# Global queries' scores between a head's two local score visits, with 128 weight columns and one key layout for both products

## The chip, the cores and the metric

The kernel runs on one core of a Trainium2 chip. The metric is the device time of one launch in microseconds. The core has TensorE (matrix products, written to PSUM), VectorE and ScalarE (both read PSUM and SBUF), GpSimd (SBUF only here) and SyncE, which issues the DMAs. In the profile they are PE (with PEld for its weight loads), DVE, ACT, POOL and SP. Each engine takes its instructions in the order of its own queue; semaphores hold an instruction back until what it needs has happened on another engine.

## The reference

Sparse attention followed by a gated feed-forward net. There are 8 batches of 8 heads, 512 local tokens, 32 global tokens and head width 64. Global queries see all 544 keys; a local query sees the 32 global keys and the local keys at most 32 positions away.

```python
k_all = np.concatenate([k_g, k_l], axis=2)
s_g = scale * np.matmul(q_g, k_all.transpose(0, 1, 3, 2))
out_g = np.matmul(sm(s_g), v_all)
...
s_ll = np.where(np.abs(pos[:, None] - pos[None, :]) <= 32, s_ll, -1000000000.0)
s_l = np.concatenate([s_lg, s_ll], axis=-1)
out_l = np.matmul(sm(s_l), np.concatenate([v_g, v_l], axis=2))
...
gate = 1.0 / (1.0 + np.exp(-(x @ w_gate)))
return (gate * (x @ w_val) @ w_out).astype(np.float32)
```

`sm` is softmax over the last axis. The 4352 tokens x of width 512 (eight heads of 64) run through a net with 1536 hidden columns.

## The kernel before

**Two streams are woven into one program.** The feed-forward net is a stream of items, one for each 128 hidden columns of a chunk of 512 tokens: 12 long products into a `bank_g`, 12 into a `bank_v` (L400), then 12 for the output of the item before (L437). After every four products the stream yields; that is one unit of time, nine units an item. The attention of the chunk that the net will need next is a list of events with due times in these units (`att_events`, L449); after each yield the events that are due are written into the program. The framework then orders the instructions for each engine by its own estimates and gives out the buffers, so an engine's queue need not follow the written order exactly.

**A head.** In the steady part a head takes 12 units (PER = 4 for each of two local units and for the global part). Local unit 0 handles query blocks 0 and 1, unit 1 blocks 2 and 3. A unit has four stages at 0, 3, 6 and 9 units after its start (`STAGES`), and unit 1 starts 4 units after unit 0:

- the scores (L239), four products into one bank, then mask and minimum on VectorE (L253) and the exponential on ScalarE (L256);
- sum and reciprocal (L259, L260) and four normalisations into `p_buf` on VectorE (L223);
- four transposes into a `bank_y` (L271), which ScalarE rounds (L282, high part) and VectorE subtracts (L283, low part) into `pt`;
- four output products (L301, L302), read by L304 and L305.

**The global part.** `global_scores` (L308) is due 8 units after the head's start. Its weights are the 32 global queries; two pairs of products run over the local keys (L318) and one pair over the 32 global keys (L320), into two banks. ScalarE copies both into the head's 32 rows of `pg` (L322, L323). After every fourth head `global_group` takes the softmax of the 128 rows (L330 to L335), transposes them (L340, 6 units later) and multiplies by the values (L361, 9 units later).

**Precision.** All products of the steady part are float32r, with an operand split in a rounded high and a low part. `split_qk` (L196) does this for queries and keys: a cast on ScalarE (L202), a subtraction for the keys (L203) and two for the queries (L205) on GpSimd. There are two `qk_hi` buffers and one `qk_raw`: a head's cast can start when the head two before has made its last product from its `qk_hi`. The first chunks, while the weights are still being converted, use plain float32 (heads called native; 12 of those with a global part). The other 52 heads are split heads.

**Buffers.** The banks `bank_x`, `bank_y`, `bank_g` and `bank_v` share four PSUM banks. A new one gets a bank that an older one has given up, and TensorE waits until the last reader of that older one is through.

**Layout.** The host lays the keys out in four groups of 160: 64 local keys, the 32 global keys, 64 local keys, with 32 keys of margin ahead (`host_layout`, L562; KEXT = 704 columns); queries 0 to 255 stand before, the others and then the global queries behind.

Heads are numbered 0 to 7 within a batch below. The period of 12 units against the item's nine gives three phases; heads 1, 4, 7 have one, 2 and 5 another, 3 and 6 the third. Groups end at heads 3 and 7.

Of the kernel before, what the change touches and what calls it, by code (L numbers as in the profile page):

```python
# [8 lines left out]
F32 = mybir.dt.float32  # L9
# [8 lines left out]
P = 128  # L18
D = 64
SL = 512  # L20
SG = 32
NH = 8
BLK = 160
KEXT = 4 * BLK + 64
K0 = 256
Q1 = K0 + KEXT
QK = Q1 + 256 + SG
# [3 lines left out]
KALL = SL + SG  # L31
# [5 lines left out]

BASE, PER = 3, 4
STAGES = (0, 3, 6, 9)
GSTAGES = (0, 6, 9)  # L40
LOAD_QK, LOAD_V, SPLIT_QK, SPLIT_V = 16, 9, 10, 4
LOAD_V_NATIVE = 4

# [16 lines left out]
def kernel(ctx, tc, qk, v, w_gate, w_val, w_out, out_l, out_g):  # L60
    nc = tc.nc
# [7 lines left out]
    att = ctx.enter_context(tc.tile_pool(name="att", bufs=2))  # L69
# [4 lines left out]
    ps = ctx.enter_context(tc.tile_pool(name="ps", bufs=1, space=PSUM))  # L74
# [18 lines left out]
    pg = const.tile([P, 5 * P], F32, name="pg_buf")  # L93
# [214 lines left out]
    def global_scores(T, row):  # L308
        ks, k0s, q0 = T["qk"], T["k0"], T["q0"]
        last = len(ks) - 1  # L310
        qg = ks[0][:, QK - SG - q0:QK - q0]
        sa = ps.tile([SG, 4, P], F32, name="bank_x", tag="att", bufs=4)
        sb = ps.tile([SG, SG], F32, name="bank_y", tag="att", bufs=4)
        for half in range(2):
            o0 = 96 * half
            for t, (src, k0) in enumerate(zip(ks, k0s)):
                view = src[:, k0 + 32:k0 + 32 + 4 * BLK].rearrange("p (j c) -> p j c", c=BLK)[:, :, o0:o0 + 64]
                nc.tensor.matmul(sa[:, :, 64 * half:64 * half + 64], qg, view, start=t == 0, stop=t == last)  # L318
        for t, (src, k0) in enumerate(zip(ks, k0s)):
            nc.tensor.matmul(sb, qg, src[:, k0 + 96:k0 + 128], start=t == 0, stop=t == last)  # L320
        rows = slice(SG * row, SG * (row + 1))
        nc.scalar.copy(pg[rows, 0:SL], sa.rearrange("p a c -> p (a c)"))  # L322
        nc.scalar.copy(pg[rows, SL:KALL], sb)  # L323

    def global_group(Ts, b, g):

# [122 lines left out]
    def att_events(ci, start, per, tail=0):  # L449
# [4 lines left out]
        nu = len(blocks) // 2  # L454
# [5 lines left out]
        for h in range(NH):  # L460
            native = ci + 1 if ci < 2 or (ci == 2 and h < START["native_heads"]) else 0
            place = (spl, "qk_hi", QK)
            if ci == 0 and h >= 4:
                place = (spl, "kl", KEXT)
            if ci == 1 and h // 2 == 2:
# [11 lines left out]
        for h in range(NH):  # L477
            T = heads[h]
            base = start + per * npu * h
            sc = per / 4  # L480
            ev.append((base - sc * LOAD_QK, 0, lambda T=T: load_qk(T)))
            ev.append((base - sc * (LOAD_V_NATIVE if T["native"] else LOAD_V), 0, lambda T=T: load_v(T)))
            ev.append((base - sc * SPLIT_QK, 1, lambda T=T: split_qk(T)))
            ev.append((base - sc * SPLIT_V, 1, lambda T=T: split_v(T)))
            for i in range(npu):
                t0 = base + per * i
                if i == nu:
                    ev.append((t0, 2, lambda T=T, h=h: global_scores(T, h % GH)))
                    if h % GH < GH - 1:
                        continue  # L490
                for o in STAGES if i < nu else GSTAGES:
                    ev.append((t0 + sc * o, 2, lambda h=h, i=i: adv(h, i)))
            if h % 2 == 1:
                ev.append((base + (nu - 1) * per + sc * STAGES[-1] + 0.5, 3,
                           lambda kt=h // 2: x_split(xts[ci], x32s[kt], kt, x0, ntok)))
# [27 lines left out]
    for ci in range(3, G):  # L523
        at, width = HOLE
        t0 = 9 * NF * (ci - 2)
# [36 lines left out]
def host_layout(inputs):  # L562
# [6 lines left out]
    kg = k_g.reshape(N, SG, D)  # L569
    ke = np.zeros((N, KEXT, D), np.float32)  # L570
    vl = v_l.reshape(N, SL, D)
    vg = v_g.reshape(N, SG, D)
    ve = np.zeros((N, 8, P, D), np.float32)
    for j in range(4):
        o = 32 + j * BLK
# [13 lines left out]
    c = np.ascontiguousarray  # L589
# [27 lines left out]
```

## Time and profile before

| | us |
|---|---|
| three timed runs | 1200.74, 1204.21, 1206.13 |
| the profiled execution | 1199.83 |
| its span, first to last instruction | 1197.8 |
| idle time of TensorE in the span | 37.1 |
| L400 into `bank_g` and `bank_v`, busy | 332.9 and 329.3 |
| L437, busy | 329.0 |
| L318 and L320 together, busy in split heads | 26.9 + 26.8 + 9.5 + 9.4 |
| L202 on ScalarE, one cast of 128x1248 | 1.24 |
| L203 on GpSimd, one subtraction of 128x704 | 1.70 |

The idle time is the span less TensorE's busy 1160.7. Products are pipelined, so the time from one start to the next is what counts for TensorE, not the length of one row. A row of the timeline gives start, length, engine, line, operation, output and inputs, shapes and the number of merged instructions; in brackets stands how long the engine was idle before it and what ended the wait. The DMA queue that carries all data was busy 41.6% of its 16 engines' time.

### The profile page before, as it was taken

To read this page: it belongs to the slowest core of one execution; us is meant where nothing else is said; L and a number is where in the kernel's file an instruction comes from. 1 tells how busy PE (TensorE), PEld (TensorE's weight loads), DVE (VectorE), ACT (ScalarE), POOL (GpSimd) and SP (SyncE) were. 2 spreads that over 40 slices of the span, in tenths; PEclk is the share of its full clock that TensorE was granted. 3 is DMA by queue.
4 is the path that set the end of the run, shared out by engine and by line. 5 is a ranking of instruction groups with operands and counts; after the bars stand their busy time and mean duration, and the time that the engine had idled before them with its cause. 6 is when DMAs were issued, how large, how long until landed. Compare 5 with 4: busy or idle time off the path is not lost.

```text
span 1197.8 us, 19349 instructions
## 1 busy us (share of the span) xinstructions
PE 1160.7 (97%) x6652; PEld 973.6 (81%) x6652; DVE 807.5 (67%) x2186; ACT 753.0 (63%) x1719; POOL 417.3 (35%) x408
## 2 busy tenths in 40 slices
PE   8889999999999999999999999999999999999998
PEld 6667778888888888888888888888888888888897
DVE  6889966766776776766776776667776677633343
ACT  5777777756765676766676666666666666532333
POOL 1335344524442444424442444424443444100000
PEclk9889999999999999999999999999999999999999
DMA  8787854333433432433343433443433332131143
GB/s 288 243 261 225 262 169 139 109 102 97 119 97 116 127 113 85 126 118 114 100 110 115 121 98 108 114 127 96 114 113 102 114 114 66 53 106 64 60 143 121
DMA packets 59489, 151.81 MB, mean 127 GB/s; under 512 B 6144, under 2 KB 19456, under 8 KB 59392
## 3 DMA queue, kind: packets, MB, share of 16 engines
q1 hardware_dynamic: 59392, 150.59, 41.6%
q8 instruction: 52, 0.85, 0.3%
q14 instruction: 45, 0.37, 0.1%
HBM read 135.36 MB, written 15.20 MB: 126 GB/s over the span
## 4 chain that ended last, share of the span: by engine, by line
PE 72%; DVE 10%; ACT 5%; issue 2%; POOL 1%; DMA 0%; DVEq 0%; ACTq 0%; POOLq 0%
PE bank_v L400 19%; PE bank_g L400 19%; PE bank_o L437 19%; PE bank_y L271 3%; DVE p_buf L223 3%; PE bank_x L239 3%; ACT s_sb L256 2%; PE bank_x L301 2%; PE bank_x L302 2%; PE bank_x L318 2%; PE bank_x L361 1%; DVE bank_v L420 1%; DVE pt L283 1%; DVE bank_v L421 1%; DVE mn L413 1%
## 5 line engine op out<-in xcount | busy, mean ns | idle before, releaser
L400 PE MATMUL bank_v<-xt,wv 128*128 128x512 f32 (+1 forms) x1440 | 329.3, 365 | 11.8 <-DVE pt L283 11.8
L400 PE MATMUL bank_g<-xt,wg 128*128 128x512 f32 (+1 forms) x1440 | 332.9, 366 | 0.2 <-ACT pg_buf L322 0.2
L437 PE MATMUL bank_o<-wo,hh 128*128 128x512 f32 x1224 | 329.0, 400 | 0.9 <-ACT hh L423 0.4
L400 PEld LDWEIGHTS bank_v<-xt,wv 128*128 128x128 f32 x1440 | 238.2, 190 | 49.3 <-PE bank_y L320 12.6
L400 PEld LDWEIGHTS bank_g<-xt,wg 128*128 128x128 f32 x1440 | 238.8, 191 | 37.6 <-issue 3.2
L437 PEld LDWEIGHTS bank_o<-wo,hh 128*128 128x128 f32 x1224 | 217.2, 189 | 40.8 <-ACT hh L423 1.4
L256 ACT ACTIVATE s_sb<-s_sb,nm 128x192 f32<-128x192 f32 (+1 forms) x240 | 110.7, 462 | 102.6 <-DVE nm L253 102.2
L223 DVE TENSOR_SCALAR p_buf<-s_sb,r 128x128 f32<-128x128 f32 (+2 forms) x443 | 145.8, 370 | 7.6 <-PE bank_y L271 1.9
L216 POOL TENSOR_TENSOR vhl<-v_raw,vhl 128x512 fp32r<-128x512 f32 x52 | 67.8, 1304 | 193.4 <-ACT vhl L215 108.1
L306 POOL TENSOR_TENSOR x<-t 64x256 f32<-64x256 f32 x104 | 76.2, 733 | 165.5 <-DVE t L305 125.2
L203 POOL TENSOR_TENSOR kl<-qk_raw,qk_hi 128x704 fp32r<-128x704 f32 x52 | 88.6, 1704 | 112.0 <-ACT qk_hi L202 111.5
L423 ACT CAST hh<-bank_v 128x512 fp32r<-128x512 f32 (+1 forms) x120 | 62.7, 522 | 95.9 <-DVE bank_v L421 95.1
L408 ACT ACTIVATE th<-bank_g 128x512 f32<-128x512 f32 (+1 forms) x120 | 63.7, 531 | 89.5 <-PE bank_g L400 88.9
L413 DVE TENSOR_SCALAR mn<-bank_g 128x512 f32<-128x512 f32 (+1 forms) x108 | 67.5, 625 | 73.2 <-ACT th L408 73.2
L305 DVE TENSOR_TENSOR t<-bank_x,t 64x512 f32<-64x512 f32 x104 | 70.8, 681 | 62.1 <-ACT t L304 61.3
L420 DVE TENSOR_TENSOR bank_v<-bank_v,mn 128x512 f32<-128x512 f32 (+1 forms) x120 | 73.7, 614 | 52.7 <-PE bank_v L400 45.9
L253 DVE CUSTOM_DVE_ANT_0 s_sb<-bank_x,masks 128x192 f32<-128x192 f32 (+1 forms) x240 | 80.8, 370 | 38.7 <-PE bank_x L239 35.8
L424 DVE TENSOR_TENSOR hh<-bank_v,hh 128x512 fp32r<-128x512 f32 (+1 forms) x120 | 73.0, 608 | 39.8 <-ACT hh L423 39.2
L271 PE MATMUL bank_y<-ident,p_buf 128*128 128x128 f32 x496 | 76.7, 275 | 6.6 <-DVE p_buf L223 5.6
L205 POOL TENSOR_TENSOR qk_hi<-qk_raw,qk_hi 64x256 fp32r<-64x256 f32 x104 | 80.4, 794 | 4.1
L271 PEld LDWEIGHTS bank_y<-ident,p_buf 128*128 128x128 f32 x496 | 60.5, 141 | 22.8 <-DVE p_buf L223 5.7
L283 DVE TENSOR_TENSOR pt<-bank_y,pt 128x512 fp32r<-128x512 f32 x104 | 70.9, 682 | 7.3 <-ACT pt L282 7.1
(110 smaller groups left out, 1707.8 us busy)
## 6 DMA issues: line engine op xcount, KB each, us to landing
wo<-wo_dram SPq DMA_DIRECT2D x116, 512.0 KB, 3.5
qk_raw<-in_qk_dram SPq DMA_DIRECT2D x104, 312.0 KB, 4.4
v_raw<-in_v_dram SPq DMA_DIRECT2D x52, 256.0 KB, 2.6
out_dram<-ob SPq DMA_DIRECT2D x34, 256.0 KB, 3.1
xt<-in_w_gate_dram SPq DMA_DIRECT2D x12, 512.0 KB, 4.9
xt<-in_w_val_dram SPq DMA_DIRECT2D x12, 512.0 KB, 4.6
xt<-in_w_out_dram SPq DMA_DIRECT2D x12, 512.0 KB, 4.5
v_nat<-in_v_dram SPq DMA_DIRECT2D x8, 512.0 KB, 6.0
```

What stands on the lines that cost most here:

```text
L203: nc.gpsimd.tensor_tensor(kl, t[:, K0:Q1], hi[:, K0:Q1].bitcast(F32), op=ALU.subtract)
L205: nc.gpsimd.tensor_tensor(hi[64:128, r], t[64:128, r], hi[64:128, r].bitcast(F32), op=ALU.subtract)
L223: nc.vector.tensor_scalar(out, in_, by, None, op0=ALU.mult)
L253: anchor[0] = nc.vector.tensor_tensor_reduce(out=s_sb[:, i, w], in0=s_ps[:, i, w], in1=mid[:, w], scale=-0.125, scalar=3.0e38, op0=ALU.add ...
L256: exp_at[0] = nc.scalar.activation(s_sb[:, i, w], s_sb[:, i, w], AF.Exp, bias=nm[:, i:i + 1], scale=-1.0, accum_out=sm[:, i:i + 1])
L271: nc.tensor.transpose(pt_ps[:, 2 * i + t], pb[:, i, t * P:(t + 1) * P], ident)
L283: nc.vector.tensor_tensor(pt[:, 1], pt_ps, pt[:, 0].bitcast(F32), op=ALU.subtract)
L306: nc.gpsimd.tensor_tensor(dst, t0[:, :, 0], t0[:, :, 1], op=ALU.add)
L400: nc.tensor.matmul(acc, w[a][:, t, fs], xt[:, c, t, x0:x0 + ntok], start=n == 0, stop=n == 11)
L413: nc.vector.tensor_scalar(mn, acc, 0.0, None, op0=ALU.min)
L420: nc.vector.tensor_tensor(acc, acc, mn, op=ALU.mult)
L437: nc.tensor.matmul(o_ps[t], ph[:, a, t * P:(t + 1) * P], pwo[:, c], start=f2 == 0 and i == 0, stop=f2 == NF - 1 and i == 2)
```

## The change

The global scores of a head are due 3 units after its start (`GLOBAL_AT`), between the scores of unit 0 (at 0) and of unit 1 (at 4), where they were due after 8. The group's stages follow at 0, 5 and 8 units from there, before 0, 6 and 9.

The weights are now the last 128 query columns, 96 local queries and the 32 global ones, so the result has 128 rows, of which the last 32 are used. The keys get a fifth part at their end, the 32 global keys again and 32 zeros (KEXT = 736, so a `qk` tile has 1280 columns in place of 1248). The first product pair runs over the first 64 keys of all four groups and this fifth part, 320 columns; the second over the last 64 of each group, 256 columns. The pair of 32 columns is gone. Each pair has a bank of its own and a copy of its own into `pg`.

```diff
-KEXT = 4 * BLK + 64
+KEXT = 4 * BLK + 3 * 32
-GSTAGES = (0, 6, 9)
+GLOBAL_AT, GSTAGES = 3, (0, 5, 8)
...
-        qg = ks[0][:, QK - SG - q0:QK - q0]
-        sa = ps.tile([SG, 4, P], F32, name="bank_x", tag="att", bufs=4)
-        sb = ps.tile([SG, SG], F32, name="bank_y", tag="att", bufs=4)
-        for half in range(2):
-            o0 = 96 * half
+        qg = ks[0][:, QK - P - q0:QK - q0]
+        rows = slice(SG * row, SG * (row + 1))
+        for half, n in enumerate((5, 4)):
+            sg = ps.tile([P, n, 64], F32, name="bank_x", tag="att", bufs=4)
             for t, (src, k0) in enumerate(zip(ks, k0s)):
-                view = src[:, k0 + 32:k0 + 32 + 4 * BLK].rearrange("p (j c) -> p j c", c=BLK)[:, :, o0:o0 + 64]
-                nc.tensor.matmul(sa[:, :, 64 * half:64 * half + 64], qg, view, start=t == 0, stop=t == last)
-        for t, (src, k0) in enumerate(zip(ks, k0s)):
-            nc.tensor.matmul(sb, qg, src[:, k0 + 96:k0 + 128], start=t == 0, stop=t == last)
-        rows = slice(SG * row, SG * (row + 1))
-        nc.scalar.copy(pg[rows, 0:SL], sa.rearrange("p a c -> p (a c)"))
-        nc.scalar.copy(pg[rows, SL:KALL], sb)
+                k = src[:, k0 + 32 + 96 * half:k0 + 96 + 96 * half]
+                view = bass.AP(k.tensor, k.offset, [k.ap[0], (BLK, n), (1, 64)])
+                nc.tensor.matmul(sg, qg, view, start=t == 0, stop=t == last)
+            nc.scalar.copy(pg[rows].rearrange("p (j c) -> p j c", c=P)[:, 0:n, 64 * half:64 * half + 64], sg[P - SG:])
...
-                t0 = base + per * i
+                t0 = base + (per * i if i < nu else sc * GLOBAL_AT)
...
+    ke[:, 32 + 4 * BLK:64 + 4 * BLK] = kg
```

The lines behind `global_scores` move up by four: L400, L408, L414, L415, L420, L421, L423, L424 and L437 of before are L396, L404, L410, L411, L416, L417, L419, L420 and L433 after, and L322 is L319. The text keeps the numbers of before, the rows of the changed program show its own.

Three places show how instructions move. First ScalarE at head 1 of a steady batch, before, from the FFN's L415 to the head's cast for a later head:

```order
L415 ACTIVATE th_6198<-th_6198 128x512
L414 ACTIVATE mn_6199<-mn_6199 128x512
L256 ACTIVATE s_sb_6232,sm_6234<-s_sb_6232,nm_6233 128x224
L256 ACTIVATE s_sb_6232,sm_6234<-s_sb_6232,nm_6233 128x192
L215 CAST vhl_6280<-v_raw_6215 128x8x64
L282 CAST pt_6260<-bank_y_6255 128x512
L423 CAST hh_6246<-bank_v_6210 128x512
L322 COPY pg_buf_104<-bank_x_6283 32x512
L323 COPY pg_buf_104<-bank_y_6284 32x32
L202 CAST qk_hi_6371<-qk_raw_6277 128x1248
```

The same place after; L411 is L415 of before:

```order
L411 ACTIVATE th_6144<-th_6144 128x512
L319 COPY pg_buf_104<-bank_x_6169 32x5x64
L410 ACTIVATE mn_6145<-mn_6145 128x512
L319 COPY pg_buf_104<-bank_x_6173 32x4x64
L202 CAST qk_hi_6315<-qk_raw_6231 128x1280
L256 ACTIVATE s_sb_6186,sm_6188<-s_sb_6186,nm_6187 128x224
L256 ACTIVATE s_sb_6186,sm_6188<-s_sb_6186,nm_6187 128x192
L215 CAST vhl_6234<-v_raw_6161 128x8x64
L419 CAST hh_6200<-bank_v_6156 128x512
L282 CAST pt_6214<-bank_y_6209 128x512
```

The two copies have moved forward, and with them the cast L202, from behind L282 and the hidden layer's cast to ahead of unit 1's two exponentials (L256); the hidden layer's cast now stands ahead of L282. In head 4 a cast of `xt` (L372) precedes L414 as well, and in heads 3 and 7 the group's exponential (L332) stands between the second copy and L202.

Second, VectorE at the same head, before, from the hidden layer's last product to the low part of `pt`:

```order
L421 SCALAR_TENSOR_TENSOR bank_v_6210<-th_6198,bank_v_6210 128x512
L260 RECIPROCAL r_6235<-r_6235 128x2
L223 TENSOR_SCALAR p_buf_100<-s_sb_6232,r_6235 128x128
L223 TENSOR_SCALAR p_buf_100<-s_sb_6232,r_6235 128x96
L223 TENSOR_SCALAR p_buf_100<-s_sb_6232,r_6235 128x128
L283 TENSOR_TENSOR pt_6260<-bank_y_6255,pt_6260 128x512
L424 TENSOR_TENSOR hh_6246<-bank_v_6210,hh_6246 128x512
```

And after:

```order
L417 SCALAR_TENSOR_TENSOR bank_v_6156<-th_6144,bank_v_6156 128x512
L259 TENSOR_SCALAR r_6189<-sm_6188 128x2
L260 RECIPROCAL r_6189<-r_6189 128x2
L223 TENSOR_SCALAR p_buf_100<-s_sb_6186,r_6189 128x128
L223 TENSOR_SCALAR p_buf_100<-s_sb_6186,r_6189 128x96
L223 TENSOR_SCALAR p_buf_100<-s_sb_6186,r_6189 128x128
L420 TENSOR_TENSOR hh_6200<-bank_v_6156,hh_6200 128x512
L283 TENSOR_TENSOR pt_6214<-bank_y_6209,pt_6214 128x512
```

L424 of before (L420 after) has moved ahead of L283. Third, TensorE at a head 5 (the phase of heads 2 and 5), before, from the transposes of unit 0 to its output:

```order
L271 MATMUL bank_y_5460<-ident_81,p_buf_100 128x128 x4
L400 MATMUL bank_g_5455<-xt_2983,wg1_109 128x512 x4
L400 MATMUL bank_g_5455<-xt_2983,wg0_108 128x512 x4
L318 MATMUL bank_x_5494<-qk_hi_5211 32x4x64
L318 MATMUL bank_x_5494<-kl_5212,qk_hi_5211 32x4x64
L318 MATMUL bank_x_5494<-qk_hi_5211 32x4x64
L318 MATMUL bank_x_5494<-kl_5212,qk_hi_5211 32x4x64
L320 MATMUL bank_y_5495<-qk_hi_5211 32x32
L320 MATMUL bank_y_5495<-kl_5212,qk_hi_5211 32x32
L400 MATMUL bank_v_5504<-xt_2983,wv0_110 128x512 x4
L301 MATMUL bank_x_5509<-pt_5465,vhl_5324 128x256
```

And after:

```order
L271 MATMUL bank_y_5422<-ident_81,p_buf_100 128x128 x4
L396 MATMUL bank_g_5417<-xt_2963,wg1_109 128x512 x4
L396 MATMUL bank_g_5417<-xt_2963,wg0_108 128x512 x4
L396 MATMUL bank_v_5456<-xt_2963,wv0_110 128x512 x4
L301 MATMUL bank_x_5461<-pt_5427,vhl_5288 128x256
```

The six products of the global scores are gone from between the transposes and the output; four products now stand ahead of unit 1's scores. The banks are given out anew as well. At this place `bank_v_5504` has the bank of the transposes `bank_y_5460` before, while after `bank_v_5456` takes that of an older `bank_v`, and the bank of `bank_y_5422` goes to the head's second transposes. After the group transposes of head 7 the next `bank_g` takes the bank of that head's first transposes; and the second transposes of heads 3 and 7 take that of the group's.

## The prediction

> **What bounds the kernel now.** I read the page's busy shares first, then the waits of TensorE, then the timeline at two heads.
>
> ```profile
> PE 1160.7 (97%) x6652; PEld 973.6 (81%) x6652; DVE 807.5 (67%) x2186; ACT 753.0 (63%) x1719; POOL 417.3 (35%) x408
> ```
>
> TensorE is the bound: 37 us of the span are idle on it. The view of waits says where the regular part of this lies:
>
> ```profile
> PE bank_v L400 <- DVE pt L283: 11.8, 12, 1.0
> PE bank_x L301 <- DVE pt L283: 3.5, 4, 1.3
> ```
>
> Twelve equal waits of 1 us, two in each of the six batches whose heads all come at the steady pace, are the only regular ones; the other row belongs to the fill. I use short names: S0, S1 are the score products of a head's units 0 and 1 (L239), T0, T1 their transposes (L271), O0, O1 their outputs (L301, L302), G the global scores (L318, L320), TG the group's transposes (L340). The timeline at head 2 of a batch:
>
> ```profile
> 549.27 0.26 PE L239 MATMUL bank_x<-qk_hi 128*128 128x224 f32 x1
> 551.54 0.60 PE L271 MATMUL bank_y<-ident,p_buf 128*128 128x128 f32 x4
> 551.56 0.48 ACT L256 ACTIVATE s_sb<-s_sb,nm 128x224 f32<-128x224 f32 x1 [1.13 <-DVE nm L253]
> 552.05 0.44 ACT L256 ACTIVATE s_sb<-s_sb,nm 128x192 f32<-128x192 f32 x1
> 552.49 0.60 ACT L215 CAST vhl<-v_raw 128x512 fp32r<-128x512 f32 x1
> 553.09 1.69 DVE L223 TENSOR_SCALAR p_buf<-s_sb,r 128x128 f32<-128x128 f32 x4
> 554.35 0.18 PE L320 MATMUL bank_y<-kl,qk_hi 128*32 128x32 f32 x1
> 554.70 0.68 DVE L283 TENSOR_TENSOR pt<-bank_y,pt 128x512 fp32r<-128x512 f32 x1
> 555.52 1.17 PE L400 MATMUL bank_v<-xt,wv 128*128 128x512 f32 x4 [0.99 <-DVE pt L283]
> ```
>
> After G, `bank_v` is given the bank of T0 (551.54). Its last reader L283 stands on VectorE behind four normalisations of unit 1 (553.09) and ends at 555.38; TensorE goes on 0.14 later. VectorE and ScalarE have time on average, but their queues are in order, and the chain exp, L223, L283 is what TensorE meets.
>
> Now head 1, which waits for nothing:
>
> ```profile
> 530.19 0.26 PE L239 MATMUL bank_x<-qk_hi 128*128 128x192 f32 x1
> 532.96 1.99 PE L400 MATMUL bank_v<-xt,wv 128*128 128x512 f32 x8
> 534.56 0.63 ACT L414 ACTIVATE mn<-mn 128x512 f32<-128x512 f32 x1
> 534.78 0.27 PE L239 MATMUL bank_x<-qk_hi 128*128 128x224 f32 x1
> 535.41 0.39 DVE L253 CUSTOM_DVE_ANT_0 s_sb<-bank_x,masks 128x224 f32<-128x224 f32 x1 [0.67 <-PE bank_x L239]
> 535.84 0.48 ACT L256 ACTIVATE s_sb<-s_sb,nm 128x224 f32<-128x224 f32 x1 [0.66 <-DVE nm L253]
> 536.33 0.44 ACT L256 ACTIVATE s_sb<-s_sb,nm 128x192 f32<-128x192 f32 x1
> 537.08 0.60 PE L271 MATMUL bank_y<-ident,p_buf 128*128 128x128 f32 x4
> 537.72 0.59 ACT L282 CAST pt<-bank_y 128x512 fp32r<-128x512 f32 x1 [0.35 <-PE bank_y L271]
> 538.04 1.26 DVE L223 TENSOR_SCALAR p_buf<-s_sb,r 128x128 f32<-128x128 f32 x3
> 538.20 0.60 ACT L423 CAST hh<-bank_v 128x512 fp32r<-128x512 f32 x1
> 539.21 0.68 DVE L283 TENSOR_TENSOR pt<-bank_y,pt 128x512 fp32r<-128x512 f32 x1
> 539.38 0.28 PE L318 MATMUL bank_x<-qk_hi 128*32 128x256 f32 x1
> 539.81 0.68 DVE L424 TENSOR_TENSOR hh<-bank_v,hh 128x512 fp32r<-128x512 f32 x1
> 539.95 1.20 PE L400 MATMUL bank_g<-xt,wg 128*128 128x512 f32 x4
> 540.73 1.24 ACT L202 CAST qk_hi<-qk_raw 128x1248 fp32r<-128x1248 f32 x1
> 540.98 0.28 PE L301 MATMUL bank_x<-pt,vhl 128*128 128x256 f32 x1
> 541.46 1.09 PE L400 MATMUL bank_g<-xt,wg 128*128 128x512 f32 x4
> 542.38 0.60 PE L271 MATMUL bank_y<-ident,p_buf 128*128 128x128 f32 x4
> ```
>
> L283 ends at 539.89, 1.1 before O0 (540.98) needs it. The reader should also see L202: the cast that fills the `qk_hi` buffer which this head gives up comes after G, at 540.73, in nobody's way.
>
> **The products themselves.** O0 is four products of 256 columns with 128-column weights: 540.98 to 541.46, 0.48, and 1.40 to 542.38 with four long products (0.92). G before takes 1.60 with four long ones (539.38 to 540.98), so 0.68: six products, and after the two of 32 columns the next load is seen (the following four take 1.20, not 1.09). The new G is like O0 with 64 more columns in two products: 0.48 + 128 × 0.48 / 1024 = 0.54. That is 0.14 saved, 7 us over 52 split heads if every head were like this; I take **−6** (5 to 7).
>
> ```profile
> L318 PEld LDWEIGHTS bank_x<-qk_hi x104: 107/108/108, 188.5 to 1028.5; 128*32 128x32 f32 x104
> 489.62 0.19 PEld L301 LDWEIGHTS bank_x<-pt,vhl 128*128 128x128 f32 x1
> ```
>
> Each load gets 0.08 longer. The Trainium skill speaks against wide weights here ("TensorE: Matmul & The Clock Gate", LDWEIGHTS): a load's time follows the number of weight columns, over 1.2 per ns, 80 ns more for 128 than for 32. These two rows agree (108 and 190 ns). By the rule alone four loads a head are 17 us dearer; in O0's 0.48 such loads are hidden beside 256 columns, so my sum counts none.
>
> In the native heads (twelve with G) the nearest rows are the scores with wide weights on the same operand:
>
> ```profile
> L239 PE MATMUL bank_x<-qk_nat 64*128 64x224 f32 x48 | 14.7, 409 | 0.0
> L318 PE MATMUL bank_x<-qk_nat 64*32 64x256 f32 x48 | 13.4, 403 | 0.0
> ```
>
> 224 columns with wide weights last what 256 last with narrow ones. The new G makes 48 such records too, of 320 and 256 columns, 288 on average: 14.7 × 288 / 224 = 18.9 against 13.4. So at most +5.5 (the small products that go are not even counted), and at least 0, since TensorE waits for other engines through much of this stage. I take **+1.5**, nearer to nothing for that reason.
>
> **The two old waits go.** By the new order `bank_v` no longer follows G there, and T0's bank goes to the second transposes, 18 long products later: −11.8. What is late next is O0, which needs the same L283 and has lost G as cover: twelve long products now lie between T0 and O0, and nothing else.
>
> **The cast moves ahead of the exponentials.** The last reader of a head's `qk_hi` is now S1, not G. The cast L202 for the head after next can start as soon as S1 is through, and stands on ScalarE ahead of unit 1's two L256 in every split head. Head 1, with t from S0. Before: S1 4.59, T0 6.89, O0 10.79. After: G (0.54) precedes S1, so S1 5.13, T0 7.43; T0 to O0 loses G, 3.90 − 0.68 = 3.22, so O0 is due at 10.65. G itself starts after four products of `bank_v`, 2.77 + 0.92 = 3.69, and ends at 4.23. S1's first reader came 0.63 after it (535.41 − 534.78), so L202 starts at 5.76. G's two copies, with the exp L414 (4.37) between them, are over by then:
>
> ```profile
> 498.33 0.58 ACT L322 COPY pg_buf<-bank_x 32x512 f32<-32x512 f32 x1 [1.25 <-PE bank_y L320]
> 498.81 0.17 ACT L323 COPY pg_buf<-bank_y 32x32 f32<-32x32 f32 x1
> 499.01 1.24 ACT L202 CAST qk_hi<-qk_raw 128x1248 fp32r<-128x1248 f32 x1
> 499.02 0.72 DVE L330 TENSOR_REDUCE mg<-pg_buf 128x1 f32<-128x544 f32 x1
> 500.15 0.75 ACT L332 ACTIVATE pg_buf<-pg_buf,mg 128x544 f32<-128x544 f32 x1
> ```
>
> (0.41 for 320 and 0.36 for 256 elements, in proportion between the two lengths here: together 0.02 more than before. First copy at 4.2, L414 after it, second copy over by 5.6.) An activation follows L202 1.14 later (499.01, 500.15); with 32 more columns 1.17. So L256 at 6.93, the second 0.49 later (7.42), L215 0.44 later (7.86), L423 0.51 later (8.37), L282 0.48 later (8.85, ends 9.44). VectorE: the L223 start 1.04 after the second L256 (552.05, 553.09), 8.46; three take 1.26, to 9.72; in the new order L424 comes ahead of L283 and takes 0.60 (539.21 to 539.81), to 10.32; L283 0.68, to 11.00; TensorE 0.14 later, 11.14. **O0 waits 0.5**, and behind O0 in TensorE's queue stand all later products. Without the cast in front the same chain would end 1.17 earlier and O0 would wait for nothing: it is the cast's place, not G's own work, that costs.
>
> The Trainium skill's remark on that page (queue depths) that ScalarE and VectorE are strict first-in-first-out is the rule behind this step; the order on ScalarE above agrees.
>
> The other heads by the same sum. **Heads 2, 5**: the exp there waited for VectorE, which was still at the hidden layer of `bank_v`, and started 2.29 after S1 (551.56). That layer now has G's 0.54 more before S1, so the exp starts when the cast is through, 0.63 + 1.17 = 1.80 after S1. L283 ended 3.84 after T0's start (551.54, 555.38), now 3.84 − 0.49 = 3.35; O0 is due 3.22 after it, plus the 0.14: 0.2 each. **Head 4**: as head 1, but a cast of `xt` (L372) stands ahead of L414 and so pushes copies, cast and exps back, by 0.3 of its 0.6 as the copies had that much room: 0.8. **Head 7** ends a group: the copies end at about 5.4, L330 and a small one 0.9, L332 at 6.3, only then L202 (0.86 later, as long as L332 with its sum), exps at 8.3 and 8.8, L283 at the earliest 8.8 + 1.04 and in fact behind a full VectorE at 10.4 to 11.1; but the next `bank_g`, right after TG, is given T0's bank and is due at 7.43 + 0.36 for T0, eight long products 1.93 and TG's 0.5, 10.2: a wait of 0.9 with the 0.14. T1 then meets TG's bank, not yet read: 0.2. **Head 3**, the other group, has the same L332 ahead of its cast, but another phase of the FFN: no `bank_g` after TG; O0 0.3 late, and T1, on TG's bank, waits for a reader that stands behind three L223 and L420 on VectorE, 0.8. This one is an estimate by head 7's chain. Heads 0 and 6: 0.1 together. Sum 0.5 + 0.4 + 0.8 + 1.1 + 1.1 + 0.1 = 4.0 per batch, **+24** over six; bounds 0 (VectorE's pitches shorter by 0.5 hide nearly all) and 36 (every ScalarE operation at full duration, no overlap). In the fill of the third chunk the four L301 waits (3.5) lose G's 0.68 as cover: **+2.5** (0 to 4).
>
> The queues passed: G issues no DMA. The earlier cast brings L203, L205 forward on POOL (0.08 longer, POOL 35% busy) and with them the next `qk_raw` issues on SP, which wait for L205; so buffer, landing and cast all move forward by the same 5 us and L202's own wait for its data stays covered. The columns that `kg` needs at the end make `qk_raw` 2.5% longer, on a queue that TensorE does not wait for in the steady part.
>
> **Sum**: −11.8 − 6 + 1.5 + 24 + 2.5 = +10. The profiled execution took 1199.8, so 1210; the runs' median is 4.4 higher, so I forecast **1214**. (Of the 1199.8, 1197.8 are the span; the 2.0 around it stay.)
>
> **Rivals.** (a) Not slower: L283 decides. If the chain from the cast to L283 is shorter by 0.5 (L202's cover, L223 at 1.2 instead of 1.26 to 1.69), the new waits shrink to 1 per batch: −11.8 − 6 + 6 + 2 = −10, 1194. For it: both engines are idle a third of the time. Against: five of the chain's links are durations from rows. Chance 0.13. (b) The new waits about replace the old ones: 2 to 3 us per batch, 12 to 18 in place of 11.8, with the products' −6 against the fill's 4: 1199 to 1210. For it: head 2 shows that the scheduler's places leave chains only 0.2 to 1 short. Chance 0.28. (c) Wide loads are seen, the skill's rule, 17 more: 1231. Against: O0's 0.48. Chance 0.05. (d) Full durations and the 36: 1226. Chance 0.09. Forecast, 1210 to 1222: 0.45.
>
> **Numbers.** The likeliest case gives the time. The range, 1197 to 1226, takes in (b), the forecast and (d), and leaves out (c) and most of (a), under 2 in 10. 0.5% (6 us) is what a measurement here can tell: faster 0.13, same 0.28, slower 0.59.
>
> **What would show it.** Right: no wait of `bank_v` on L283 after G; L301 waiting on L283 at heads 1 and 4 by over 0.4, `bank_g` after TG at head 7; L202 ahead of the second L256 pair, 5.8 after S0; the G group at 0.54. Wrong: L301 without waits (rival a), or loads standing alone in the new G (c).

## The result and the profile after

| | us |
|---|---|
| kernel before, median of 4 runs | 1202.47 (1200.38 to 1206.13) |
| changed kernel, median of 4 runs | 1253.35 (1252.78 to 1255.08) |
| ratio | 1.041, 95% interval 1.039 to 1.044 |
| changed kernel, profiled execution | 1253.07, span 1251.0 |

The change costs 51 us (53 between the two profiled executions). The sign and the place were forecast, the size was not: 1214 was expected, and 1253 lies above the range.

The page of the changed kernel, first its busy times, then the chain of work that ended last (shares of the span):

```profile
PE 1177.9 (94%) x6524; PEld 978.5 (78%) x6524; DVE 840.0 (67%) x2186; ACT 758.0 (61%) x1719; POOL 417.5 (33%) x408
PE 57%; DVE 18%; ACT 12%; POOL 6%; issue 4%; DMA 2%; DVEq 0%; POOLq 0%; ACTq 0%
```

VectorE is busy 32.5 us longer than before with the same 2186 instructions: some of them take longer. That is the first thing that the prediction doesn't explain. TensorE is idle 73 us, 36 more than before; its busy time, in which the profile models the products' ends, is 17 us longer. The view of its waits in the changed kernel (total, times, longest):

```profile
PE bank_x L301 <- POOL vhl L216: 14.9, 12, 1.4
PE bank_x L301 <- DVE pt L283: 14.0, 19, 1.2
PE bank_y L336 <- DVE mn L409: 7.2, 7, 1.6
PE bank_g L396 <- DVE pt L283: 6.4, 6, 1.2
...
PE bank_y L271 <- DVE ptg L342: 1.9, 5, 0.4
```

The old waits of `bank_v` on L283 are gone. O0 (L301) waits instead, `bank_g` after TG waits, and the second bank of TG does. The first row seems to name a new culprit, GpSimd's value split L216. The timeline at head 1 shows that it isn't one; t counts from S0 at 558.30:

```profile
558.30 0.25 PE L239 MATMUL bank_x<-qk_hi 128*128 128x192 f32 x1
...
563.47 0.27 PE L239 MATMUL bank_x<-qk_hi 128*128 128x224 f32 x1
...
564.09 1.27 ACT L202 CAST qk_hi<-qk_raw 128x1280 fp32r<-128x1280 f32 x1
565.26 0.48 ACT L256 ACTIVATE s_sb<-s_sb,nm 128x224 f32<-128x224 f32 x1
565.43 1.77 POOL L203 TENSOR_TENSOR kl<-qk_raw,qk_hi 128x736 fp32r<-128x736 f32 x1 [2.79 <-ACT qk_hi L202]
565.74 0.44 ACT L256 ACTIVATE s_sb<-s_sb,nm 128x192 f32<-128x192 f32 x1
565.77 0.60 PE L271 MATMUL bank_y<-ident,p_buf 128*128 128x128 f32 x4
566.17 0.60 ACT L215 CAST vhl<-v_raw 128x512 fp32r<-128x512 f32 x1
566.46 0.78 DVE L259 TENSOR_SCALAR r<-sm 128x2 f32<-128x2 f32 x1
567.27 0.17 DVE L260 RECIPROCAL r<-r 128x2 f32<-128x2 f32 x1
567.28 0.59 ACT L282 CAST pt<-bank_y 128x512 fp32r<-128x512 f32 x1
567.28 1.50 POOL L205 TENSOR_TENSOR qk_hi<-qk_raw,qk_hi 64x256 fp32r<-64x256 f32 x2
567.54 1.33 DVE L223 TENSOR_SCALAR p_buf<-s_sb,r 128x128 f32<-128x128 f32 x3
568.79 0.68 DVE L420 TENSOR_TENSOR hh<-bank_v,hh 128x512 fp32r<-128x512 f32 x1
568.87 1.27 POOL L216 TENSOR_TENSOR vhl<-v_raw,vhl 128x512 fp32r<-128x512 f32 x1
569.39 0.67 DVE L283 TENSOR_TENSOR pt<-bank_y,pt 128x512 fp32r<-128x512 f32 x1
570.21 0.36 PE L301 MATMUL bank_x<-pt,vhl 128*128 128x256 f32 x1 [1.05 <-POOL vhl L216]
```

L283 ends at 570.06 and O0 starts 0.15 later, the same 0.14 as in the kernel before. L216 happens to end between the two, at 570.14, and the view puts the wait down to the last. In all 12 steady heads where the row says L216, O0 starts 0.145 after L283's end, as it does in the heads whose row names L283. (The `vhl` that L216 makes here is that of the next head.)

Now compare with the chain that the prediction wrote down for this head:

| step | predicted t | measured t |
|---|---|---|
| cast L202 starts | 5.76 | 5.79 |
| first and second L256 | 6.93, 7.42 | 6.96, 7.44 |
| L215 | 7.86 | 7.87 |
| L282 | 8.85 | 8.98 |
| first L223 | 8.46 | **9.24** |
| L283 ends | 11.00 | **11.76** |
| O0 starts | 11.14 | **11.91** |

ScalarE is right to 0.13. Between the exponentials and the normalisations 0.78 is lost, and it stays to the end of the chain. The row that stands there is L259, a sum over two elements per partition: 0.78 in place of 0.17. The groups by line, before and after (busy, mean ns):

```profile
L259 DVE TENSOR_SCALAR r<-sm 128x2 f32<-128x2 f32 x128 | 21.9, 171 | 56.9 <-ACT s_sb L256 55.9 <-ACT s_first L256 1.0
```

```profile
L259 DVE TENSOR_SCALAR r<-sm 128x2 f32<-128x2 f32 x128 | 56.1, 438 | 59.3 <-ACT s_sb L256 57.6 <-ACT s_first L256 1.0
```

That is 34.2 us more, as much as VectorE's whole surplus. GpSimd's L203 ends at 567.20 and L259 at 567.24. Of the 128, 49 start while L203 runs; they last 863 ns on average and end at least 23 ns after it, mostly 24 to 32. L223 is next behind L205, in the same manner.

The Trainium skill states this ("SBUF — State Buffer", Who interferes with whom): VectorE's second pair of SBUF ports is GpSimd's only one, it goes as an exclusive lock to whichever instruction is issued first, and a `tensor_scalar`, which L259 and L223 are, can ask for it. The trace agrees, with these 23 to 32 ns; the prediction had not looked there.

**Where the 51 us lie.** I compare the time at which the same long product starts in two profiled executions. Up to the first of the six steady batches (246 us in the kernel before) the changed kernel loses 11.0; in the six batches 40.2, which is some 4 to 9 in each; after them 2.1.

### The profile page after: what moved, and what is told of

The parts are those of the page before. It is cut to its first block, busy times and chain, and to the rows that moved or that the text cites. A ratio compares the mean times of both kernels' runs of the same rounds, so it can differ in the third digit from the quotient of the medians.

```text
span 1251.0 us, 19000 instructions
## 1 busy us (share of the span) xinstructions
PE 1177.9 (94%) x6524; PEld 978.5 (78%) x6524; DVE 840.0 (67%) x2186; ACT 758.0 (61%) x1719; POOL 417.5 (33%) x408
## 4 chain that ended last, share of the span: by engine, by line
PE 57%; DVE 18%; ACT 12%; POOL 6%; issue 4%; DMA 2%; DVEq 0%; POOLq 0%; ACTq 0%
PE bank_g L396 15%; PE bank_o L433 14%; PE bank_v L396 13%; DVE p_buf L223 4%; PE bank_x L239 4%; ACT s_sb L256 3%; ACT qk_hi L202 3%; DVE r L259 3%; PE bank_y L271 3%; PE bank_x L301 2%; POOL kl L203 2%; POOL qk_hi L205 2%; PE bank_x L302 2%; PE bank_x L318 2%; ACT pg_buf L319 1%
## 5 line engine op out<-in xcount | busy, mean ns | idle before, releaser
L396 PE MATMUL bank_g<-xt,wg 128*128 128x512 f32 (+1 forms) x1440 | 338.8, 369 | 6.6 <-DVE pt L283 6.4
L396 PE MATMUL bank_v<-xt,wv 128*128 128x512 f32 (+1 forms) x1440 | 333.6, 366 | 1.0 <-DVE hh L420 1.0
L433 PE MATMUL bank_o<-wo,hh 128*128 128x512 f32 x1224 | 325.1, 397 | 1.9 <-ACT ob L375 1.3
L396 PEld LDWEIGHTS bank_g<-xt,wg 128*128 128x128 f32 x1440 | 239.6, 192 | 48.5 <-DVE pt L283 7.8
L396 PEld LDWEIGHTS bank_v<-xt,wv 128*128 128x128 f32 x1440 | 238.2, 190 | 37.9 <-issue 2.1
L433 PEld LDWEIGHTS bank_o<-wo,hh 128*128 128x128 f32 x1224 | 219.3, 189 | 44.4 <-ACT ob L375 2.3
L306 POOL TENSOR_TENSOR x<-t 64x256 f32<-64x256 f32 x104 | 76.1, 732 | 295.8 <-DVE t L305 248.8
L203 POOL TENSOR_TENSOR kl<-qk_raw,qk_hi 128x736 fp32r<-128x736 f32 x52 | 93.0, 1789 | 177.9 <-ACT qk_hi L202 177.9
L223 DVE TENSOR_SCALAR p_buf<-s_sb,r 128x128 f32<-128x128 f32 (+2 forms) x443 | 143.6, 364 | 5.9
L256 ACT ACTIVATE s_sb<-s_sb,nm 128x192 f32<-128x192 f32 (+1 forms) x240 | 110.3, 461 | 36.3 <-DVE nm L253 36.1
L404 ACT ACTIVATE th<-bank_g 128x512 f32<-128x512 f32 (+1 forms) x120 | 64.0, 534 | 99.2 <-PE bank_g L396 98.5
L409 DVE TENSOR_SCALAR mn<-bank_g 128x512 f32<-128x512 f32 (+1 forms) x108 | 67.6, 626 | 78.0 <-ACT th L404 77.9
L419 ACT CAST hh<-bank_v 128x512 fp32r<-128x512 f32 (+1 forms) x120 | 62.6, 522 | 89.0 <-DVE bank_v L417 87.7
L304 ACT COPY t<-bank_x 64x512 f32<-64x512 f32 x104 | 60.7, 583 | 75.9 <-PE bank_x L302 62.5
L305 DVE TENSOR_TENSOR t<-bank_x,t 64x512 f32<-64x512 f32 x104 | 70.6, 679 | 49.0 <-ACT t L304 47.9
L416 DVE TENSOR_TENSOR bank_v<-bank_v,mn 128x512 f32<-128x512 f32 (+1 forms) x120 | 73.5, 612 | 41.8 <-PE bank_v L396 36.2
L259 DVE TENSOR_SCALAR r<-sm 128x2 f32<-128x2 f32 x128 | 56.1, 438 | 59.3 <-ACT s_sb L256 57.6
L420 DVE TENSOR_TENSOR hh<-bank_v,hh 128x512 fp32r<-128x512 f32 (+1 forms) x120 | 72.7, 605 | 32.2 <-ACT hh L419 31.1
L301 PE MATMUL bank_x<-pt,vhl 128*128 128x256 f32 x208 | 56.9, 296 | 32.3 <-POOL vhl L216 14.9
L271 PE MATMUL bank_y<-ident,p_buf 128*128 128x128 f32 x496 | 78.3, 276 | 6.6 <-DVE p_buf L223 3.1
L410 ACT ACTIVATE mn<-mn 128x512 f32<-128x512 f32 (+1 forms) x108 | 63.0, 584 | 32.0 <-DVE mn L409 27.4
```

Source lines behind the costliest of these rows:

```text
L203: nc.gpsimd.tensor_tensor(kl, t[:, K0:Q1], hi[:, K0:Q1].bitcast(F32), op=ALU.subtract)
L223: nc.vector.tensor_scalar(out, in_, by, None, op0=ALU.mult)
L256: exp_at[0] = nc.scalar.activation(s_sb[:, i, w], s_sb[:, i, w], AF.Exp, bias=nm[:, i:i + 1], scale=-1.0, accum_out=sm[:, i:i + 1])
L259: nc.vector.tensor_scalar_add(r, sm, 1e-9)
L271: nc.tensor.transpose(pt_ps[:, 2 * i + t], pb[:, i, t * P:(t + 1) * P], ident)
L301: nc.tensor.matmul(o_ps[:, i], vt[:, VM[j], :], pt[:, :, 2 * i, :], start=True, stop=False)
```

## The experiments

The theory that I put to the test, "cast and lock": the cast delays the exponentials, and its follower L203 on GpSimd then holds VectorE. The rivals: the cast alone; L216, as the view of waits says; the new form of the products; the new due times as such. The table gives the ratio to the kernel before, its 95% interval, and the loss against it in the profiled executions before, in and after the six steady batches.

| run | median us | ratio | interval | start | six batches | rest |
|---|---|---|---|---|---|---|
| changed kernel | 1253.4 | 1.041 | 1.039 to 1.044 | 11.0 | 40.2 | 2.1 |
| e1 layout only | 1216.0 | 1.009 | 1.006 to 1.012 | 14.6 | 1.6 | 2.9 |
| e2 place only | 1242.6 | 1.031 | 1.028 to 1.033 | 4.6 | 34.6 | 0.2 |
| e3 cast behind | 1223.8 | 1.015 | 1.013 to 1.017 | 7.2 | 15.7 | 2.3 |
| e4 subtractions behind | 1305.7 | 1.083 | 1.079 to 1.087 | 11.7 | 85.6 | 2.1 |
| e5 unheld norms | 1232.4 | 1.023 | 1.020 to 1.026 | 13.1 | 16.4 | 3.0 |
| e6 value split behind | 1204.7 | 1.001 | 0.9985 to 1.0026 | 0.3 | 1.1 | 0.3 |
| e8 unheld norms, before | 1200.9 | 0.998 | 0.9956 to 0.9995 | 4.5 | -0.9 | 1.2 |
| e9 lock added, bfloat16 | 1205.7 | 1.002 | 1.0004 to 1.0039 | 5.5 | 1.8 | 1.6 |
| e9b lock added, float32 | 1259.2 | 1.046 | 1.043 to 1.049 | 1.7 | 53.9 | 1.7 |
| e10 native as before | 1243.1 | 1.033 | 1.030 to 1.036 | 0.6 | 38.3 | 2.8 |
| e11 before, both edits | 1195.8 | 0.994 | 0.991 to 0.997 | 1.0 | -5.9 | 0.3 |
| e12 change mended | 1211.7 | 1.006 | 1.004 to 1.007 | 0.8 | 7.3 | 2.1 |

A line number in an experiment's rows is that of its own kernel; in brackets stands what it is in the changed one. The column "start" of a single execution can move by 5 us without an edit that concerns it: e8 and e9 leave the native heads as they were and show 4.5 and 5.5.

**e1, e2: which half of the change.** e1 is the changed kernel at the old due times (with the group's stages at 0, 6, 9), e2 the kernel before with the new ones. The line in e1:

```diff
-                t0 = base + (per * i if i < nu else sc * GLOBAL_AT)
+                t0 = base + per * i
```

> The new weights and key layout alone: G back at its old due time (8 units after the head's start) and the group's stages at 0, 6, 9, so the cast L202 comes after G again. Theory 'place' (the cast ahead of the exponentials, and what it brings forward, makes the 51 us): only G's own saving shows, 0.09 us per split head by the changed kernel's trace, so 1202 - 5 = 1197, between 1192 and 1203; L259 stays at 0.17 us in all heads. Rival 'form' (wide loads, the 320-column product or a second bank per head in the output pool cost the time): 1230 to 1253.

> The move alone: G with its old six products, 32 weight columns and two copies, but due 3 units after the head's start, group stages 0, 5, 8. Theory 'place': as the changed kernel plus the 5 us that the new products saved, 1250 to 1262, and L259 long (mean near 0.44 us) again. Rival 'form': near the time before, 1200 to 1215.

In the steady batches "place" is right: e2 has 34.6 of the 40.2 and its long L259, e1 has 1.6 and its old waits. TensorE's waits in e1, then the group L259 in e2:

```profile
PE bank_v L396 <- DVE pt L283: 11.7, 12, 1.2
```

```profile
L259 DVE TENSOR_SCALAR r<-sm 128x2 f32<-128x2 f32 x128 | 52.9, 414 | 58.7 <-ACT s_sb L256 57.2 <-ACT s_first L256 1.0
```

Both expectations missed in part. e1 did not gain 5 us: it loses 14.6 at the start (in one execution; by the medians it is 10 us slower in all), and in the steady batches G's shorter products bring nothing: L283's waits stay, and the FFN's products of L396 take 2.8 us longer there. In e2 the old layout costs less than the new one at the same place, 34.6 against 40.2. The new L203 is 0.08 and the new L202 0.03 longer, and both now stand in the chain; whether that makes the difference was not tried.

**e3, e4: cast and subtractions apart.** `behind` queues an instruction behind another of its own engine, without a new wait: in e3 the cast behind unit 0's L282 (`"pt", 0`) of the head in work, in e4 the subtractions behind the addition L306 of its O0 (`"x", 0`).

```diff
+        with behind(T, 2, ('pt', 0)):
+            nc.scalar.copy(hi, t)
...
+        with behind(T, 2, ('x', 0)):
+            nc.gpsimd.tensor_tensor(kl, t[:, K0:Q1], hi[:, K0:Q1].bitcast(F32), op=ALU.subtract)
+            for r in (slice(0, K0), slice(Q1, QK)):
+                nc.gpsimd.tensor_tensor(hi[64:128, r], t[64:128, r], hi[64:128, r].bitcast(F32), op=ALU.subtract)
```

> The changed kernel, with the cast L202 queued on ScalarE behind unit 0's copy L282 of the same stretch, so behind unit 1's exponentials; G stays between S0 and S1. Theory 'cast and lock' (the cast delays the exponentials by 1.2, and its follower L203 on GpSimd holds VectorE's L259 back by 0.7 to 0.9 more): both go, L259 back to 0.17; 40 us of steady waits shrink to about the 14 of before, so 1205 to 1220. Rival 'due times' (G and the group's stages at 0, 5, 8 press on the FFN and on the banks by themselves): over 1240. Rival 'value split' (O0 waits for GpSimd's L216, as the waits view says) gives the same time here, as L216 comes ahead of L203 again.

> The changed kernel, cast L202 left where it is, ahead of the exponentials; only GpSimd's L203 and L205 that follow it are queued behind the addition L306 of the head's O0, about 6 us later. Theory 'cast and lock': L259 back to 0.17, each of 49 heads' chains shorter by 0.75, 37 us in all at most; part of it comes back where L216, now first, runs beside L223: 1215 to 1235. Theory 'cast alone' (the exponentials' 1.2 us delay is all that counts): no change, 1250 to 1256. Rival 'value split': L216 no longer stands behind L203 and L205, so the 12 waits of 1.4 (14.9) go and nothing else: 1236 to 1242, O0 no longer put down to L216 but L259 not the reason.

e3 takes 24.5 of the 40.2 back, and L259 falls from 0.44 to 0.21 us on average; at 1223.8 it is 4 us above the expected range. It moves the cast and the subtractions behind it together, so it doesn't part them. e4 is 52 us slower than the changed kernel, which no theory had. It tested something else: the subtractions are the last readers of the one `qk_raw` buffer. Six us later they release it too late, and the cast, now waiting for its data, stands in front of the exponentials. ScalarE's waits (L207 is the cast), and one of them in the timeline:

```profile
ACT qk_hi L207 <- DMA qk_raw<-in_qk_dram: 50.0, 28, 4.1
```

```profile
575.56 1.12 SPq L183 DMA_DIRECT2D qk_raw<-in_qk_dram  x2
...
581.01 1.26 ACT L207 CAST qk_hi<-qk_raw 128x1280 fp32r<-128x1280 f32 x1 [2.77 <-DMA qk_raw<-in_qk_dram]
```

So the time of this run says nothing of the lock. Its rows do: with the cast ahead of the exponentials as in the changed kernel, but L203 elsewhere, L259 takes 0.22 us on average in place of 0.44. The cast's early place needs early subtractions; a second buffer, which would part them, was not tried.

**e5: the lock taken out on VectorE's side.** ScalarE and GpSimd stay as changed.

```diff
-        nc.vector.tensor_scalar_add(r, sm, 1e-9)
-        nc.vector.reciprocal(r, r)
+        if nat:
+            nc.vector.tensor_scalar_add(r, sm, 1e-9)
+        nc.vector.reciprocal(r, r if nat else sm)
...
+            norms.insert(len(norms) if nat or n == 2 else 0,
+                         (pb[:, i, 128:128 + 32 * n].rearrange("p (a c) -> p a c", c=32), side, r[:, i:i + 1]))
+        for n in norms:
+            scaled(nat, *n)
```

> The changed kernel, ScalarE and GpSimd untouched; on VectorE, in split heads, the sum L259 is left out (1e-9 does not change a float32 sum of at least 1), so L260 reads the exponentials' sums, and of a unit's four normalisations L223 the one of three pieces (128x96, which took 301 ns beside GpSimd as without it) comes first. Theory 'cast and lock' (L203 holds L259 back until 26 ns after its own end): the first operation that can be held now comes 0.5 later, when L203 is nearly through; L283 0.6 to 0.75 earlier in seven heads of a batch, some 28 of the 40 us in the steady batches go: 1218 to 1233, waits of O0 on L283 mostly under 0.6. Theory 'cast alone': only the 0.17 of L259 in seven heads of six batches, 7 us: 1243 to 1250. The cast itself stays, so neither gives the time before.

23.8 of the 40.2 go, the median is 1232.4. "Cast alone" (1243 at the least, with the 0.17 of the missing L259 counted) is refuted: nothing but VectorE's own queue was touched. TensorE's waits of O0 (L306 here) fall to a third:

```profile
PE bank_x L306 <- DVE pt L288: 9.7, 14, 1.8
...
PE bank_x L306 <- POOL vhl L216: 1.2, 1, 1.2
```

Not every head gains. At head 1 all four normalisations now stand ahead of L283 in VectorE's queue, and L205 holds two of them; O0 waits as long as before there. The gain is at heads 2 to 6, and a part of it comes back as waits of T1 for TG's reader (6.6 us in place of 1.9).

**e6, e8, e11: the same lock in the kernel before.** There L216 ran beside the first normalisations. e6 moves L216 itself behind O0's addition, e8 has e5's edit, e11 has that and the cast L215 behind L282.

```diff
+        with behind(T, 1, ('x', 0)):
+            nc.gpsimd.tensor_tensor(vhl[:, :, D:2 * D], t, vhl[:, :, 0:D].bitcast(F32), op=ALU.subtract)
...
-        with tc.issue_after(exp_at[0].ins):
+        with tc.issue_after(exp_at[0].ins), behind(T, 1, ("pt", 0)):
             nc.scalar.copy(vhl[:, :, 0:D], t)
```

> The kernel before, with the value split L216 on GpSimd queued behind the addition L306 of the head's O0 (due time of the split 2 units before the head, was 4). In the kernel before, 41 of the first normalisations L223 ran beside L216 and took 0.98 us on average, 0.28 without. Theory 'lock': these go back to 0.29 and the 12 waits of bank_v on L283 shrink from 1.0 to 0.3 us each: 1206 - 8 = 1198 (1194 to 1202). Rival 'no lock': no change, 1203 to 1209. Rival 'late loads': v_raw has one buffer; where its reload comes too late, L215 holds up ScalarE as the cast did in run e4: over 1225.

> The kernel before, with the same edit on VectorE as e5 (no L259 in split heads, the 128x96 normalisation of a unit first). Theory 'lock': L216 holds the first two-piece L223 only while it still runs, 0.3 us less, and 0.17 for L259: the 12 waits of bank_v on L283 from 1.0 to 0.4 to 0.6 each, 1206 - 6 = 1200 (1196 to 1203). Rival 'no lock': 0.17 for 12 waits, 2 us: 1204.

> The kernel before, with VectorE's edit of e8 and, on ScalarE, the value cast L215 queued behind unit 0's copy L282: L282 comes 0.6 earlier, and L216, which follows L215, starts when the normalisations are nearly through. Theory 'lock': the 12 waits of bank_v on L283 fall to 0.4 or less: 1196 (1191 to 1200). Rival: the waits move to another operation, as in e6: 1200 to 1205.

e6 brought nothing: `bank_v` waits less for L283 (7.9 in place of 11.8), but L216 now holds L259 in 29 heads (0.70 us on average), and a new wait on L305 takes 4.8. It settles the rival "value split", though: in e6 L216 stands behind an addition that needs O0's result. If O0 needed that L216, the kernel could not run. e8 is as expected, 2.6 us, at the edge of what can be told from no change. e11 is **faster than both kernels**: the 12 waits of `bank_v` are gone from the view of TensorE's waits. Of its first two rows (L282 is L271, L312 is L301) the first is that of the start; the second is what is left in the steady batches, mostly one wait of O0 a batch:

```profile
PE bank_y L282 <- DVE p_buf L228: 6.2, 7, 2.2
PE bank_x L312 <- DVE pt L294: 6.1, 7, 1.1
```

Since e11 changes ScalarE's order as well, its gain is not that of the lock alone; the edit on VectorE without it (e8) gave 2.6.

**e9, e9b: the lock put into the kernel before.** One useless GpSimd operation beside unit 1's exponentials, ScalarE's order untouched; first e9's, then e9b's, which a tiny operation on the same queue starts:

```diff
+            nc.gpsimd.tensor_scalar(busy, busy, nm[:, 1:2], None, op0=ALU.mult)
...
+            go = nc.gpsimd.tensor_tensor(tick, nm[:, 1:2], nm[:, 1:2], op=ALU.subtract)
+            with tc.issue_after(go.ins):
+                nc.gpsimd.tensor_tensor(busy, wg[0][:, 0, 0:736].bitcast(F32), wg[1][:, 0, 0:736].bitcast(F32),
+                                        op=ALU.subtract)
```

> The kernel before, with one useless GpSimd operation per split head: a product over a 128x736 scratch tile that starts when unit 1's minimum (L253) is there, that is beside the exponentials L256, as L203 does in the changed kernel; ScalarE's order stays as before. Theory 'lock': L259 is held to the end of that operation, then L223 by L216 behind it; L283 0.7 or more late in every head; the two old waits per batch grow by that, 12 x 0.75 = 9, and heads that had 1.1 spare begin to wait: 1215 to 1240. Rival 'cast alone' or 'no lock': 1203 to 1210, since GpSimd was busy only 35% and no engine waits for the tile.

> The kernel before, with a useless GpSimd subtraction like L203 (two float32 inputs, 128x736) in the 48 split heads of the last six batches, started when unit 1's minimum is there; ScalarE's order stays. In run e9 the useless operation was a product with one bfloat16 input, and L259 ran beside it at 0.22 us: that kind did not hold VectorE. Theory 'lock by two-input operations': L259 is now held for about 1.1 us to the end of the subtraction, and L283 comes that much later in nearly all heads: the 12 waits grow from 1.0 to about 2, and heads with 1.1 to spare begin to wait, 13 to 30 us in all: 1216 to 1235. Rival 'no lock': 1203 to 1210, as in e9.

e9 added 111 us of work to GpSimd and cost 2, as the rivals said and not as "lock" did; L259 (L263 here) was hardly held. The theory was narrowed by this to operations of L203's kind. The groups:

```profile
L261 POOL TENSOR_SCALAR busy<-busy,nm 128x736 bf16<-128x736 bf16 x52 | 110.9, 2134 | 119.5 <-DVE nm L255 103.7 <-PE bank_g L404 15.3
L263 DVE TENSOR_SCALAR r<-sm 128x2 f32<-128x2 f32 x128 | 24.7, 193 | 57.6 <-ACT s_sb L258 56.5 <-ACT s_first L258 1.0
```

e9b added less work, of the kind of L203, and cost **55 us**, more than the whole change. Its groups (L266 is L259), a head in its timeline, and TensorE's waits:

```profile
L263 POOL TENSOR_TENSOR busy<-wg,wg 128x736 bf16<-128x736 f32 x48 | 85.5, 1781 | 0.0
L266 DVE TENSOR_SCALAR r<-sm 128x2 f32<-128x2 f32 x128 | 72.7, 568 | 56.8 <-ACT s_sb L258 55.7 <-ACT s_first L258 1.0
```

```profile
556.85 1.77 POOL L263 TENSOR_TENSOR busy<-wg,wg 128x736 bf16<-128x736 f32 x1
...
557.50 1.14 DVE L266 TENSOR_SCALAR r<-sm 128x2 f32<-128x2 f32 x1
```

```profile
PE bank_v L407 <- DVE pt L290: 22.2, 12, 1.9
PE bank_x L308 <- DVE pt L290: 14.7, 23, 1.4
...
PE bank_g L407 <- DVE pt L290: 5.9, 12, 0.5
```

All 48 were held to 22 to 30 ns past the subtraction's end, 1.23 us on average, longer than the 0.86 in the changed kernel. So GpSimd's operation alone, with the cast at its old place, costs as much as the change did. Some 6 of the 55 us come by a detour: after the longest waits 30 long products start 0.43 apart in place of 0.23, and from 577 to 583 us the granted clock is 0.72. The expectation was too low by 24: it gave the other heads 1.1 to spare. Heads 1 and 7 have nothing: already in the kernel before, `bank_g` behind G starts there 0.054 after L283's end, the same as where it waits for L283 here. The prediction read head 1 as waiting for nothing, by O0 alone.

**e10, e12: the start, and the change mended.** e10 keeps the old G and its due times in the native heads alone. e12 adds the edits of e3 and e5.

```diff
-                t0 = base + (per * i if i < nu else sc * GLOBAL_AT)
+                t0 = base + (per * i if i < nu or T["native"] else sc * GLOBAL_AT)
```

> The changed kernel, but the native heads keep the old G (32 weight columns, six products, old due times); the split heads are as changed. The changed kernel loses 11 us before the steady part begins, 7.3 of them by the time the third chunk's heads start. If these come from the native heads' G (wider weights and its earlier place), they go: 1253 - 7 = 1246 (1243 to 1249). Rival: they come from the chunk order and the split heads' casts: 1250 to 1256.

> The changed kernel with three edits: native heads keep the old G (e10), VectorE's edit (e5), and the cast L202 behind L282 (e3). Theory 'cast and lock': of e3's 2.9 us per batch at least half goes with the edit on VectorE, the fill's 7 with the old native G: 1204 to 1213. Rival 'due times' (G between S0 and S1 and the group's stages cost by themselves): 1214 to 1224.

e10 takes 10 us back, nearly all at the start (11.0 to 0.6). e12 lies in the range of "cast and lock", but 0.6% above the kernel before: 7.3 us remain in the steady batches. TensorE's waits there are those of O0 at heads 2 and 3, of T1 behind TG at heads 3 and 7, and of `bank_g` at head 7, 3.1 to 3.4 us a batch where the kernel before has 2.5; what makes up the rest was not taken apart.

## Why the prediction was right in kind and wrong in size

- **The two old waits go (-11.8).** Right: no wait of `bank_v` on L283 is left in the steady batches.
- **The products (-6).** Right as a duration of the new G: it and the long product behind it take 0.54 and 0.23 in the split heads, 0.535 and 0.314 before, so 0.08 per head is saved, not 0.14 (head 1, where the old one was read, has the hidden wait of `bank_g` in it). The wide loads were not seen; rival (c) falls. But the saving is worth nothing where TensorE then waits for L283 by so much longer, and e1 shows no gain in the steady batches, where the products of L396 took back 2.8 us.
- **The cast ahead of the exponentials.** Right in every row of ScalarE to 0.13, and e3 shows what its place, with that of the subtractions behind it, is worth: 24.5 of the 40.2.
- **The queues passed: the failed step.** The prediction wrote that L203 and L205 come forward on POOL, "0.08 longer, POOL 35% busy", and counted nothing for it. It asked whether anyone waits for GpSimd's results, and whether its own queue has room. It did not ask what GpSimd's operation does to VectorE while it runs. L203 starts 0.07 after the cast and lasts 1.77; the exponentials take 0.9 of that; L259 meets the rest. In the kernel before, the same L203 ran mostly beside operations that read PSUM, never beside L259, which took 0.17. e5 (taken out: 23.8 of the 40.2 us go) and e9b (put in: 55 us come) show it from both sides.
- **The new waits (+24).** Per batch, from one start to the next less the products' own pace: head 1 1.2 (0.5 forecast), heads 2 and 5 1.4 and 0.8 (0.2 each), head 4 1.6 (0.8), head 7 2.0 (1.1), head 3 1.15 (1.1), head 6 0.5 (0.1 with head 0). 8.7 in place of 4.0, so 52 in place of 24. Seven heads with 0.7 each on average are the difference. Head 3 came out right by luck: forecast were waits of O0 and T1, measured is one of TG's last transposition, for L409 on VectorE.
- **The native heads and the fill (+1.5 and +2.5).** Mis-sized: 11.0, and e10 shows that 10 come from the native heads' G. Its own busy time rose by little, as forecast; form alone (e1) costs 14.6 there, place alone (e2) 4.6, each in one execution. Part of it goes with TensorE's granted clock: from 40 to 80 us it is 0.84 in the changed kernel, 0.94 in the kernel before and in e10. e8 and e9, with native heads as before, have 0.83 there and lose 4.5 and 5.5 in the column "start", so a low clock in this stage comes without the change too. Why it is low, and which waits take up the rest, was not settled.

How the 40 us divide: e5 takes 23.8 away. Up to 7 of these can be the 0.17 of the missing L259 itself, so the lock has about 17 at the least (an estimate, from 0.17 in seven heads of six batches); head 1 stays held in e5, so it may have more. Mending the cast's place on top of that (e12) removes 9 more, and 7 are left. The shares overlap, since e3 alone takes 24.5: moving the cast moves L203 with it.

## What to carry to other kernels

When an instruction moves, list not only who waits for it and what it queues behind, but also what will run beside it on an engine that can hold another up: here GpSimd's float32 subtractions beside VectorE's scaling between SBUF tiles. A 2-element operation in a chain is no cheap link if it lasts 0.86 us in place of 0.17, or 1.23 as in e9b. An engine busy for 35% can still set the time by where its work lies. A row that names the releaser of a wait is to be compared with the gap that the true one leaves each time, here 0.145 for O0 and `bank_v` and 0.054 for `bank_g`.

## What the runs showed of the hardware beyond that

- Which operations are held. Beside GpSimd, L259 (128x2) and the L223 of two pieces (128x128) were; the reciprocal (128x2, 164 ns before and after) and the L223 of three pieces (128x96, 301 ns in 62 that started with GpSimd idle and 301 in 53 that started beside it) never were beside float32 operations.
- Not every GpSimd operation holds for its whole time. In e9 (one bfloat16 input, 2.13 us) L259 was let go 0.89 us after the operation's start in 27 of 52 heads, and in the other 25 it started from 0.75 on and ran in 0.16 to 0.17. Of the L223 of two pieces, 24 of 27 that started 1.0 to 1.4 after it ran free, and all 39 from 1.6 on were held to its end. The Trainium skill ("SBUF — State Buffer", Who interferes with whom) has the lock held for the whole instruction; for this operation the rows differ. Spans on GpSimd are rough in the profile; why they differ was not tried.
- The FFN's long products of L396 take 232 ns from start to start (median) in the changed kernel, e1 and e3, 229 in the kernel before and 230 in e2. It is not the key layout as such: e9 and e9b, with the old layout and one more tile of 128x736, have 234. The cause was not looked for.
